# Transposing attention weights on VectorE and by transfers instead of on TensorE

## The chip, the cores and the metric

The kernel runs on one core of a Trainium2 chip. Its time is the device time of one execution, in microseconds (us). Three runs of the kernel before took 1422.08, 1422.11 and 1425.74 us; the median is 1422.11 us. One execution was also profiled: every instruction on the five engines (PE is TensorE, PEld its weight loads, DVE is VectorE, ACT is ScalarE, POOL is GpSimd) and on SyncE (SP), which here only issues transfers.

## The reference

Three layers follow one another. The attention pools keys and values over 8 positions, so each head has 576 queries and only 72 keys:

```
k_p = k.reshape(B, H, 72, 8, D).mean(axis=3)        # B = 8, H = 8, D = 64
v_p = v.reshape(B, H, 72, 8, D).mean(axis=3)
scores = (q @ k_p.T) / 8
attn = exp(scores - scores.max(-1)); attn = attn / (attn.sum(-1) + 1e-9)
x = attn @ v_p                                       # then 4608 tokens x 512
x = softplus(x @ w_in) @ w_out                       # 512 -> 2048 -> 512
# then: tokens with x @ w_skip > 0 go through one of 8 experts (512 -> 1024 -> 512),
# weighted by its gate, and are added to x; the others pass unchanged
```

## The kernel before, in words

**Groups.** The 4608 tokens are worked in nine groups of 512 (`NG = 9`, `G = 512`). A batch has 576 tokens, so a group holds a piece of one batch or pieces of two: 64 + 448 tokens in group 1, 128 + 384 in group 2, 192 + 320 in group 3, and so on to 448 + 64 in group 7; groups 0 and 8 lie in one batch. For group g the main loop (L738 to L765) goes through 16 columns c of the hidden layer: `p1` makes twelve matmuls `h` of 512 columns (L665) and the softplus on ACT and DVE, `p2`, two columns later, makes twelve matmuls `y` (L686 to L688). Matmuls are split into a high and a low part, three where one would do.

**Units.** The attention of group g + 1 is worked beside the main loop of group g, in four units, one per pair of heads. A unit is a generator (`unit`, L518); each `yield` ends one of its steps. `Feed.tick` (L645) advances every unit that runs by one step; it is called twice per column c, so a tick is twelve matmuls long, and a new unit starts every six ticks. The steps of a unit: load queries `q` and keys `k` (L533, L534); two ticks later pool the keys (L543), copy them into the two diagonal blocks of `kbd` (L550, L551), and multiply: scores `s` (L554) have queries on the partitions, up to six tiles of 64 to 128 queries per unit, each 144 wide (72 keys of two heads). DVE takes maxima and subtracts (L567, L568), ACT makes the exponential (L574), DVE sums and inverts (L575 to L577), POOL multiplies (L578). This lies in `q`'s own buffer. Then the weights have to stand with the keys on the partitions, as the product with the values needs them: PE transposes each tile and head into PSUM (`tr`, L606) and ACT copies the two halves to `et` (L608). Two ticks later PE makes `o` (L614), which ACT and DVE split into `xh` and `xl` (L616, L617). The values are pooled (L589) and transposed (`pv`, L595) on the way.

**Order.** A scheduler turns the program into one fixed list per engine; each engine works its list in order, so an instruction that waits holds up all behind it. SP's list holds all plain transfers: `k`, `q`, `v`, the gating rows `w9b` (L103), which wait for buffers that DVE's products `junk` (L118) free, and the stores `x2d` of finished rows (L155), which wait for the gate that DVE and POOL make at the end of `finish` (L106). `junk`, nine per row tile, 36 per group, runs beside the units of the second next group. There are two buffers for `q`, one each for `kv`, `et` and `vr`, and two PSUM banks (`ps_a`) for `s`, `pv`, `tr` and `o`.

**The tail.** After the last group the experts are worked in blocks of 256 rows (L803 on). There each block's rows are turned by DVE in 32x32 blocks and by 16 transfers from SBUF to SBUF (`spread`, L375 to L383), the only place of this kernel that does so.

Of the kernel before, what the change touches and what calls it, by code (L numbers as in the profile page):

```python
# [9 lines left out]
F32 = mybir.dt.float32  # L10
# [4 lines left out]
AF = mybir.ActivationFunctionType  # L15
ALU = mybir.AluOpType
AX = mybir.AxisListType
# [3 lines left out]
P = 128  # L21
# [4 lines left out]
SP = 72  # L26
G = 512
T = G // 128
# [6 lines left out]
def tile_kernel(ctx, tc, qT, kT, vT, wbits, w9, w1, w2, out):  # L35
    nc = tc.nc
# [23 lines left out]
    ident = const.tile([P, P], F32, name="ident")  # L60
# [358 lines left out]
    with ExitStack() as ph:  # L419
        pp = ph.enter_context(tc.tile_pool(name="pp", bufs=5))  # L420
# [6 lines left out]
        ps_a = ph.enter_context(tc.tile_pool(name="ps_a", bufs=2, space=PSUM))  # L427
# [3 lines left out]
        kbd = []  # L431
        for i in range(2):
            t = ep.tile([P, 2 * SP], F32, name=f"kbd{i}")
# [80 lines left out]

        pooled = {}
        count = [0]

        def unit(hp, part, xh, xl, first):  # L518

            pieces, n = [], 0  # L520
            for b, r0, rn, c0 in part:
                nt = -(-rn // P)
                if rn % nt:
                    nt += 1
                pieces.append((b * 4 + hp, r0, rn, c0, nt, rn // nt, n))
                n += nt
            assert n <= 6
            qe = room("q", G if first else 12 * SP, first)
            k = None
            for u, r0, rn, c0, nt, tp, n0 in pieces:  # L530
                if u not in pooled:
                    k = room("kv", 576, first)
                    nc.sync.dma_start(out=k, in_=kT[u])  # L533
                nc.sync.dma_start(out=qe[:, c0:c0 + rn], in_=qT[u, :, r0:r0 + rn])  # L534
            yield
            yield

            banks = [ps_a.tile([P, 512], F32, tag="pa", name="s") for _ in range(-(-n // 3))]
            parts = []
            for u, r0, rn, c0, nt, tp, n0 in pieces:  # L540
                if u not in pooled:
                    kp = pp.tile([P, SP], F32, tag="kp", name="kp")
                    nc.vector.tensor_reduce(kp, k.rearrange("p (s w) -> p s w", w=8), AX.X, ALU.add)  # L543
                    v = room("kv", 576, first)
                    nc.sync.dma_start(out=v, in_=vT[u])
                    pooled[u] = (kp, v, None)
                kp = pooled[u][0]
                kb = kbd[count[0] % 2]
                count[0] += 1
                nc.scalar.activation(out=kb[0:64, 0:SP], in_=kp[0:64, :], func=AF.Copy)  # L550
                nc.scalar.activation(out=kb[64:128, SP:2 * SP], in_=kp[64:128, :], func=AF.Copy)  # L551
                for t in range(nt):
                    i = n0 + t
                    nc.tensor.matmul(banks[i // 3][:tp, i % 3 * 144:(i % 3 + 1) * 144],  # L554
                                     lhsT=qe[:, c0 + t * tp:c0 + (t + 1) * tp], rhs=kb, start=True, stop=True)
                i = n0
                while i < n0 + nt:
                    j = min(n0 + nt, (i // 3 + 1) * 3)
                    parts.append((i, j, tp))
                    i = j  # L560
            e = (k if first else qe)[:, :n * 2 * SP].rearrange("p (a k) -> p a k", k=SP)
            st = room("st", 24 if first else 36, first)
            mx, sm, rc = (st[:, i * 2 * n:(i + 1) * 2 * n] for i in range(3))
            for i, j, tp in parts:
                s3 = banks[i // 3][:tp, i % 3 * 144:(i % 3 + j - i) * 144].rearrange("p (a k) -> p a k", k=SP)
                m = mx[:tp, 2 * i:2 * j]
                nc.vector.tensor_reduce(m, s3, AX.X, ALU.max)  # L567
                nc.vector.tensor_tensor(out=e[:tp, 2 * i:2 * j], in0=s3,  # L568
                                        in1=m.unsqueeze(2).to_broadcast([tp, 2 * (j - i), SP]),
                                        op=ALU.subtract)  # L570
            for u, r0, rn, c0, nt, tp, n0 in pieces:
                h = slice(2 * n0, 2 * (n0 + nt))
                ep_ = e[:tp, h]
                nc.scalar.activation(out=ep_, in_=ep_, func=AF.Exp, scale=1.0 / 64)  # L574
                nc.vector.tensor_reduce(sm[:tp, h], ep_, AX.X, ALU.add)  # L575
                nc.vector.tensor_scalar_add(sm[:tp, h], sm[:tp, h], 1e-9)
                nc.vector.reciprocal(rc[:tp, h], sm[:tp, h])  # L577
                nc.gpsimd.tensor_tensor(out=ep_, in0=ep_, op=ALU.mult,  # L578
                                        in1=rc[:tp, h].unsqueeze(2).to_broadcast([tp, 2 * nt, SP]))
            yield  # L580
            yield
            if not first:
                yield
            vr = None
            for u, *_ in pieces:
                kp, v, vp = pooled[u]
                if vp is None:
                    vr = room("vr", SP, first)
                    nc.vector.tensor_reduce(vr, v.rearrange("p (s w) -> p s w", w=8), AX.X, ALU.add)  # L589
            yield  # L590
            for u, *_ in pieces:
# [7 lines left out]
            if not first:  # L599
                yield  # L600
            et = room("et", 2 * G, first).rearrange("p (a k) -> p a k", a=2)[:SP]
            for h in range(2):
                tr = ps_a.tile([P, 512], F32, tag="pa", name="tr")
                for u, r0, rn, c0, nt, tp, n0 in pieces:
                    for t in range(nt):
                        nc.tensor.transpose(tr[:SP, c0 + t * tp:c0 + (t + 1) * tp],  # L606
                                            e[:tp, 2 * (n0 + t) + h, :], ident[:tp, :tp])
                nc.scalar.activation(out=et[:, h, :], in_=tr[:SP, :], func=AF.Copy)  # L608
            yield
            yield  # L610
            o = ps_a.tile([P, 512], F32, tag="pa", name="o")
            for u, r0, rn, c0, nt, tp, n0 in pieces:
# [4 lines left out]
            nc.vector.scalar_tensor_tensor(out=xl[:, hp, :], in0=o, scalar=0.125,  # L617
                                           in1=xh[:, hp, :].bitcast(F32), op0=ALU.mult, op1=ALU.subtract)

        X = {}  # L620

        def units_of(g):
            xh = xp.tile([P, 4, G], F32R, tag="xh", name="xh")
            xl = xp.tile([P, 4, G], F32R, tag="xl", name="xl")
            X[g] = (xh, xl)
            part = []
            t0 = g * G
            while t0 < (g + 1) * G:
                n = min((g + 1) * G, (t0 // 576 + 1) * 576) - t0
                part.append((t0 // 576, t0 % 576, n, t0 - g * G))  # L630
                t0 += n
            return [unit(hp, part, xh, xl, g == 0) for hp in range(4)]

        jobs, ends = [], []

# [142 lines left out]
        t = xp.tile([P, 4 * G], F32, tag="xl", name="xg1")  # L778
# [4 lines left out]
        g = NG - 1  # L783
# [171 lines left out]
```

## Time and profile before

| | |
|---|---|
| median of three runs | 1422.11 us (1422.08 to 1425.74) |
| the profiled execution | 1414.45 us, span of its instructions 1412.6 us |
| granted TensorE clock, mean over the span | 0.993 of full speed |
| busy in the span | PE 97%, PEld 81%, DVE 61%, ACT 45%, POOL 23% |
| transfers | 124.73 MB in 70752 packets |

The span is the time from the first to the last instruction of the profiled execution; 1.85 us lie around it. Its time is 7.66 us under the median of the three runs. Each row of a view gives an engine, a line of the kernel, the operation, the tiles as out<-in, the shapes and times; a wait is named by what ended it. A matmul's own duration holds its passage through the array, so that the durations of matmuls overlap: what one costs is read from the distance of starts.

### The profile page before, as it was taken

Reading aid. Unit: us, or ns where it says so; the run is one execution under the profiler, and the core shown is the slowest. Engines: PE = TensorE matmul, PEld = TensorE weight load, DVE = VectorE, ACT = ScalarE, POOL = GpSimd, SP = SyncE. Lnnn points to the kernel's source line nnn. Section 1 sums busy time; section 2 is a strip of 40 time slices with the busy share of each in tenths; the row PEclk is TensorE's granted clock in tenths of the full one; section 3 lists DMA queues with packets and bytes.
Section 4 is the critical chain, followed back from the end, with each engine's and each line's share of the span. In section 5 each row is a group of like instructions: output and inputs, shape, how many; then the busy total and the mean of one; then the engine's idle time right before and its main releaser. Section 6 shows DMA issues by size and latency. Waiting matters only on the chain. (4 is left out here: it accounts for less than half of the span.)

```text
span 1412.6 us, 21524 instructions
## 1 busy us (share of the span) xinstructions
PE 1366.5 (97%) x7290; PEld 1137.4 (81%) x7290; DVE 861.7 (61%) x2055; ACT 639.6 (45%) x1168; POOL 322.7 (23%) x370
## 2 busy tenths in 40 slices
PE   5899999999999999999999999999999999999986
PEld 3667877787877888778778878888998998989985
DVE  7897684784783883973963954844563532326263
ACT  6986555545554554555555454462111111114141
POOL 2011021021111121121121020234342443424332
PEclk9999999999999999999999999999999999999998
DMA  8813131131140230230220210423323222324272
GB/s 290 300 63 92 56 108 41 55 108 33 55 117 25 60 111 25 71 100 26 82 73 9 75 38 11 146 76 89 99 79 98 65 65 65 90 63 168 65 271 70
DMA packets 70752, 124.73 MB, mean 88 GB/s; under 512 B 21941, under 2 KB 37941, under 8 KB 68064
## 3 DMA queue, kind: packets, MB, share of 16 engines
q1 hardware_dynamic: 52896, 86.05, 19.7%
q0 software_dynamic: 17728, 37.13, 8.3%
q8 instruction: 61, 1.00, 0.3%
q14 instruction: 67, 0.55, 0.1%
HBM read 166.67 MB, written 29.67 MB: 139 GB/s over the span
## 5 line engine op out<-in xcount | busy, mean ns | idle before, releaser
L665 PE MATMUL h<-xh,wt 128*128 128x512 f32 x1152 | 388.5, 398 | 5.6 <-DVE a L671 5.0
L665 PEld LDWEIGHTS h<-xh,wt 128*128 128x128 f32 x1152 | 216.4, 188 | 62.9 <-issue 11.0
L118 DVE CUSTOM_DVE_ANT_0 junk<-rows,w9b 128x512 bf16<-128x512 f32 x324 | 234.4, 723 | 9.3 <-ACT rows L112 3.7
L838 PE MATMUL h<-xt,w1h 128*128 128x256 f32 x1280 | 227.9, 282 | 3.8 <-ACT w1h L403 3.0
L686 PE MATMUL y<-wt,gh 128*128 128x512 f32 x576 | 229.7, 399 | 0.0
L665 PE MATMUL h<-xl,wt 128*128 128x512 f32 x576 | 226.1, 392 | 0.0
L688 PE MATMUL y<-wt,gl 128*128 128x512 f32 x576 | 224.7, 390 | 0.0
L687 PE MATMUL y<-wt,gh 128*128 128x512 f32 x576 | 224.5, 390 | 0.0
L671 DVE SCALAR_TENSOR_TENSOR a<-h,a 128x512 f32<-128x512 f32 x144 | 99.0, 687 | 174.6 <-ACT a L670 174.4
L838 PEld LDWEIGHTS h<-xt,w1h 128*128 128x128 f32 x1280 | 197.5, 189 | 6.2 <-ACT w1h L403 3.8
L668 ACT ACTIVATE a<-h 128x512 f32<-128x512 f32 x144 | 86.1, 598 | 233.3 <-PE h L665 208.9
L578 POOL TENSOR_TENSOR q<-q,st 64x144 f32<-64x144 f32 (+7 forms) x60 | 64.2, 1078 | 541.0 <-DVE st L577 167.6
L842 ACT ACTIVATE hs<-h 128x512 fp32r<-128x512 f32 x80 | 47.5, 598 | 298.6 <-PE h L838 224.2
L838 PE MATMUL h<-xt,w1l 128*128 128x256 f32 x640 | 180.4, 282 | 1.4 <-DVE w1l L404 0.8
L673 ACT ACTIVATE gh<-a 128x512 fp32r<-128x512 f32 x144 | 91.0, 632 | 125.0 <-DVE a L671 124.4
L686 PEld LDWEIGHTS y<-wt,gh 128*128 128x128 f32 x576 | 108.2, 188 | 24.9 <-issue 1.0
L665 PEld LDWEIGHTS h<-xl,wt 128*128 128x128 f32 x576 | 108.5, 188 | 23.5 <-issue 2.9
L688 PEld LDWEIGHTS y<-wt,gl 128*128 128x128 f32 x576 | 108.1, 188 | 23.4 <-issue 0.7
L675 DVE TENSOR_TENSOR gl<-a,gh 128x512 fp32r<-128x512 f32 x144 | 100.2, 696 | 40.6 <-ACT gh L673 39.8
L687 PEld LDWEIGHTS y<-wt,gh 128*128 128x128 f32 x576 | 108.3, 188 | 20.6
L838 PEld LDWEIGHTS h<-xt,w1l 128*128 128x128 f32 x640 | 122.9, 192 | 1.8 <-DVE w1l L404 1.0
L864 PE MATMUL y<-w2h,hs 128*128 128x512 f32 x304 | 118.4, 390 | 1.2 <-DVE hs L843 1.2
(191 smaller groups left out, 1907.1 us busy)
## 6 DMA issues: line engine op xcount, KB each, us to landing
w9b<-w SPq DMA_DIRECT2D x81, 256.0 KB
raw<-wbits SPq DMA_DIRECT2D x12, 1024.0 KB
x2d<-rows SPq DMA_DIRECT2D x36, 260.0 KB
kv<-kT SPq DMA_DIRECT2D x28, 288.0 KB
kv<-vT SPq DMA_DIRECT2D x28, 288.0 KB
xm<-misc SPq DMA_DIRECT2D x160, 32.0 KB
misc<-misc SPq DMA_DIRECT2D x144, 32.0 KB
raw<-wbits SPq DMA_DIRECT2D x8, 512.0 KB
```

The costliest lines, as they stand in the source:

```text
L118: nc.vector.tensor_tensor_reduce(out=ws["junk"], in0=rows[t][:, :D], in1=w9b[e], scale=1.0, scalar=0.0, op0=ALU.mult, op1=ALU.add, accum_o ...
L578: nc.gpsimd.tensor_tensor(out=ep_, in0=ep_, op=ALU.mult, in1=rc[:tp, h].unsqueeze(2).to_broadcast([tp, 2 * nt, SP]))
L665: nc.tensor.matmul(h, lhsT=l, rhs=r[:, kk, :], start=n == 0, stop=n == 11)
L668: nc.scalar.activation(out=a, in_=h, func=AF.Abs)
L671: nc.vector.scalar_tensor_tensor(out=a, in0=h, scalar=0.0, in1=a, op0=ALU.max, op1=ALU.add)
L673: nc.scalar.activation(out=gh, in_=a, func=AF.Copy)
L675: nc.vector.tensor_tensor(out=gl, in0=a, in1=gh.bitcast(F32), op=ALU.subtract)
L686: nc.tensor.matmul(y, lhsT=th, rhs=wh, start=c == 0, stop=False)
L687: nc.tensor.matmul(y, lhsT=th, rhs=wl, start=False, stop=False)
L688: nc.tensor.matmul(y, lhsT=tl, rhs=wh, start=False, stop=c == 15)
L838: nc.tensor.matmul(h[:, f2, :], lhsT=l, rhs=r[:, kk, :], start=n == 0, stop=n == 11)
L864: nc.tensor.matmul(y, lhsT=hl[:, f, js], rhs=ws["w2h"][:, f, :], start=False, stop=f == 7)
```

## The change

Group 0 keeps the old way (`unit0`). For groups 1 to 8 the unit works four tiles of 128 queries whatever the pieces are: where a piece ends inside a tile, that tile's scores come from two matmuls with 64 rows each. Each tile and head has 96 columns, of which 72 hold weights and POOL sets 24 to zero. DVE then transposes the whole buffer in place, in 32x32 blocks, 128 x 768 elements in one instruction. A block then has the right content on the wrong partitions, so twelve transfers per unit, issued by SP, bring blocks of the same key range to their partitions in `et`: four bands of 32 source partitions times three key ranges of 32, 32 and 8 keys, each with eight runs of 32 elements (128 bytes) per partition. PE's transposes and ACT's copies of these units are gone. The output step comes five ticks after the transposition; before it came two ticks after the transposes on PE.

```diff
-            et = room("et", 2 * G, first).rearrange("p (a k) -> p a k", a=2)[:SP]
-            for h in range(2):
-                tr = ps_a.tile([P, 512], F32, tag="pa", name="tr")
-                for u, r0, rn, c0, nt, tp, n0 in pieces:
-                    for t in range(nt):
-                        nc.tensor.transpose(tr[:SP, c0 + t * tp:c0 + (t + 1) * tp],
-                                            e[:tp, 2 * (n0 + t) + h, :], ident[:tp, :tp])
-                nc.scalar.activation(out=et[:, h, :], in_=tr[:SP, :], func=AF.Copy)
...
+        def unit(hp, us, xh, xl):
+            qe = room("q", 2 * T * 96, False)
...
+            for u, r0, rn, c0 in us:
+                kb = keys(u, k, lambda: room("kv", 576, False))
+                c = c0
+                while c < c0 + rn:
+                    t, p0 = divmod(c, P)
+                    m = min(P - p0, c0 + rn - c)
+                    nc.tensor.matmul(banks[t // 2][p0:p0 + m, t % 2 * 144:(t % 2 + 1) * 144],
+                                     lhsT=qe[:, c:c + m], rhs=kb, start=True, stop=True)
+                    c += m
...
+            e = qe.rearrange("p (a k) -> p a k", k=96)
+            nc.gpsimd.memset(e[:, :, SP:], 0.0)
+            shares(e[:, :, :SP], sm, rc)
+            yield
+            yield
+            yield
+            nc.vector.transpose(out=qe, in_=qe)
+            et = room("et", 2 * G, False)
+            src = qe.rearrange("p (a k r) -> p a k r", k=3, r=32)
+            dst = et.rearrange("p (a q r) -> p a q r", q=4, r=32)
+            for q in range(4):
+                for kb, n in enumerate((32, 32, 8)):
+                    nc.sync.dma_start(out=dst[32 * kb:32 * kb + n, :, q], in_=src[32 * q:32 * q + n, :, kb])
+            vr = room("vr", SP, False)
+            sums(us, vr)
+            yield
+            values(us, vr)
+            yield
+            yield
+            yield
+            yield
+            output(us, et.rearrange("p (a k) -> p a k", a=2)[:SP], hp, xh, xl)
```

`keys`, `shares`, `sums`, `values` and `output` hold the code of the old unit's steps, one instruction where there was one per piece.

PE's list before, in the main loop of group 2, where the first unit of group 3 is transposed (`y` and `h` are the main loop's matmuls, `tr` the transposes, those of one shape in one row):

```order
L686 MATMUL y_2403<-wt_181,gh 128x512
L687 MATMUL y_2403<-wt_181,gh 128x512
L688 MATMUL y_2403<-wt_181,gl 128x512
L606 MATMUL tr<-ident,q 72x96 x2
L606 MATMUL tr<-ident,q 72x80 x4
...
L665 MATMUL h<-xh,wt_553 128x512
L665 MATMUL h<-xl,wt_553 128x512
```

The same place in PE's list now:

```order
L721 MATMUL y_2348<-wt_181,gh 128x512
L722 MATMUL y_2348<-wt_181,gh 128x512
L723 MATMUL y_2348<-wt_181,gl 128x512
L700 MATMUL h<-xh,wt_547 128x512
L700 MATMUL h<-xl,wt_547 128x512
```

The transposes between `y` and `h` are gone and nothing of the attention stands there.

SP's list before, in the main loop of group 2, where the rows of group 1 are stored (`w9b` are gating rows, `kv` keys or values, `x2d` the stores):

```order
L103 DMA w9b<-w 128x512
L545 DMA kv<-vT 128x576
L103 DMA w9b<-w 128x512 x2
L155 DMA x2d<-rows 128x520 x4
L533 DMA kv<-kT 128x576
L534 DMA q<-qT 128x256 x2
```

The same place in SP's list now (`et` are the new transfers):

```order
L522 DMA kv<-vT 128x576
L644 DMA et<-q 32x8x32 x2
L644 DMA et<-q 8x8x32
...
L644 DMA et<-q 32x8x32
L155 DMA x2d<-rows 128x520 x4
...
L609 DMA kv<-kT 128x576
```

The four stores, which used to stand alone, now stand among the twelve transfers of one unit, the third of the group.

## Rows read from the trace of the kernel before

**Rows 1.** Busy time of the engines over the span, from the page

```profile
PE 1366.5 (97%) x7290; PEld 1137.4 (81%) x7290; DVE 861.7 (61%) x2055; ACT 639.6 (45%) x1168; POOL 322.7 (23%) x370
```

**Rows 2.** Windows view: PE, PEld, DVE, ACT, POOL busy; clock, DMA share, GB/s

```profile
150.00:200.00 50.00, 49.01 (x242) 39.57 (x241) 44.65 (x122) 28.98 (x62) 3.98 (x4) 1.00 0.26 77
```

**Rows 3.** Waits of PE: engine, line, what ended the wait, total us, times, longest

```profile
PE o L614 <- DVE q L568: 5.2, 9, 1.2
```

**Rows 4.** PE's transposes: count, shortest/median/longest ns, first and last start, forms

```profile
L606 PE MATMUL tr<-ident,q x304: 230/259/291, 54.0 to 846.2; 128*72 128x128 f32 x64, 112*72 112x112 f32 x32, 80*72 80x80 f32 x32, 96*72 96x96 f32 x16
```

**Rows 5.** Timeline of PE, twelve matmuls apart: start us, duration us, instruction

```profile
305.49 0.39 PE L686 MATMUL y<-wt,gh 128*128 128x512 f32 x1
...
308.20 0.39 PE L665 MATMUL h<-xh,wt 128*128 128x512 f32 x1
```

**Rows 6.** Timeline of PE around transposes of 8, 12 and 10 tiles

```profile
169.21 0.39 PE L688 MATMUL y<-wt,gl 128*128 128x512 f32 x1
169.44 1.03 PE L606 MATMUL tr<-ident,q 128*72 128x128 f32 x8
...
170.55 0.39 PE L665 MATMUL h<-xl,wt 128*128 128x512 f32 x1
...
313.55 0.39 PE L688 MATMUL y<-wt,gl 128*128 128x512 f32 x1
313.77 1.05 PE L606 MATMUL tr<-ident,q 96*72 96x96 f32 x12
...
314.94 0.39 PE L665 MATMUL h<-xl,wt 128*128 128x512 f32 x1
...
681.62 0.39 PE L688 MATMUL y<-wt,gl 128*128 128x512 f32 x1
681.85 1.41 PE L606 MATMUL tr<-ident,q 112*72 112x112 f32 x10
...
683.53 0.40 PE L665 MATMUL h<-xl,wt 128*128 128x512 f32 x1
```

**Rows 7.** Timeline of PE around the scores of six tiles

```profile
317.23 0.39 PE L665 MATMUL h<-xh,wt 128*128 128x512 f32 x1
317.45 1.63 PE L554 MATMUL s<-kbd,q 128*96 128x144 f32 x12
...
319.15 0.40 PE L687 MATMUL y<-wt,gh 128*128 128x512 f32 x1
```

**Rows 8.** Timeline of PE: scores of two other units

```profile
296.58 1.63 PE L554 MATMUL s<-kbd,q 128*96 128x144 f32 x12
...
379.22 1.15 PE L554 MATMUL s<-kbd,q 128*128 128x144 f32 x8
```

**Rows 9.** Timeline of POOL: the last multiplication of the same two units

```profile
304.51 3.11 POOL L578 TENSOR_TENSOR q<-q,st 96x288 f32<-96x288 f32 x2 [17.76 <-ACT xh L616]
...
386.87 0.93 POOL L578 TENSOR_TENSOR q<-q,st 128x288 f32<-128x288 f32 x1 [0.87 <-DVE st L577]
```

**Rows 10.** DVE's block transposition in the tail: busy us, mean ns, idle before

```profile
L378 DVE STREAM_TRANSPOSE misc<-xg 128x512 f32<-128x512 f32 x38 | 24.8, 690 | 14.0 <-DVEq L823 5.5 <-DMA misc<-misc 4.0 <-DMA xg<-x2d,ids 1.4
```

**Rows 11.** The tail's transfers on SP: shortest/median/longest ns of an issue

```profile
L383 SPq DMA_DIRECT2D xm<-misc x160: 507/589/2146, 991.4 to 1401.1; - x160
```

**Rows 12.** Timeline of SP: one block's 16 transfers

```profile
991.40 10.03 SPq L383 DMA_DIRECT2D xm<-misc  x16
```

**Rows 13.** A stretch in which SP issues only such transfers

```profile
1016.00:1018.00 2.00, 2.00 (x11) 1.65 (x10) 0.67 (x2) 0.00 (x0) 0.00 (x0) 1.00 0.20 53
```

**Rows 14.** Timeline at the start: first load, and who uses it

```profile
0.80 0.40 SPq L533 DMA_DIRECT2D boot_kv<-kT  x1
...
3.61 0.75 DVE L543 TENSOR_REDUCE kp<-boot_kv 128x72 f32<-128x576 f32 x1 [2.31 <-DMA boot_kv<-kT]
```

**Rows 15.** Timeline of SP: stores of a group's rows

```profile
311.22 1.80 SPq L155 DMA_DIRECT2D x2d<-rows  x4
```

**Rows 16.** The stretch in which those stores and a key load move

```profile
311.00:317.00 6.00, 6.00 (x37) 5.03 (x35) 2.96 (x7) 3.58 (x7) 2.26 (x6) 1.00 0.74 239
```

More of the change, by code (lines that the diff above doesn't have):

```diff
@@ L516, in tile_kernel @@
         count = [0]
[L518 to L529, printed above, removed]
-            for u, r0, rn, c0, nt, tp, n0 in pieces:
[L531 to L551, printed above, removed]
-                for t in range(nt):
[L553 to L585, printed above, removed]
@@ new lines, in keys @@
+        def keys(u, k, kv):
+            if u not in pooled:
+                kp = pp.tile([P, SP], F32, tag="kp", name="kp")
+                nc.vector.tensor_reduce(kp, k.rearrange("p (s w) -> p s w", w=8), AX.X, ALU.add)
+                v = kv()
+                nc.sync.dma_start(out=v, in_=vT[u])
+                pooled[u] = (kp, v, None)
+            kp = pooled[u][0]
+            kb = kbd[count[0] % 2]
+            count[0] += 1
+            nc.scalar.activation(out=kb[0:64, 0:SP], in_=kp[0:64, :], func=AF.Copy)
+            nc.scalar.activation(out=kb[64:128, SP:2 * SP], in_=kp[64:128, :], func=AF.Copy)
+            return kb
@@ L586, in unit, with shares, sums @@
+        def shares(e, sm, rc):
+            nc.scalar.activation(out=e, in_=e, func=AF.Exp, scale=1.0 / 64)
+            nc.vector.tensor_reduce(sm, e, AX.X, ALU.add)
+            nc.vector.tensor_scalar_add(sm, sm, 1e-9)
+            nc.vector.reciprocal(rc, sm)
+            nc.gpsimd.tensor_tensor(out=e, in0=e, op=ALU.mult,
+                                    in1=rc.unsqueeze(2).to_broadcast([P, 2 * T, SP]))
+        def sums(us, vr):
+            for u, *_ in us:
                 kp, v, vp = pooled[u]
@@ L587, in unit, with values @@
                 if vp is None:
-                    vr = room("vr", SP, first)
                     nc.vector.tensor_reduce(vr, v.rearrange("p (s w) -> p s w", w=8), AX.X, ALU.add)
-            yield
-            for u, *_ in pieces:
+        def values(us, vr):
+            for u, *_ in us:
                 kp, v, vp = pooled[u]
@@ L598, in unit, with output @@
                     pooled[u] = (kp, v, vp)
[L599 to L610 removed]
+        def output(us, et, hp, xh, xl):
             o = ps_a.tile([P, 512], F32, tag="pa", name="o")
[L612 removed]
+            for u, r0, rn, c0 in us:
                 for h in range(2):
@@ L618, in unit, with unit0 @@
                                            in1=xh[:, hp, :].bitcast(F32), op0=ALU.mult, op1=ALU.subtract)
+        def unit0(hp, us, xh, xl):
+            (u, r0, rn, c0), = us
+            q, k = room("q", G, True), room("kv", 576, True)
+            nc.sync.dma_start(out=k, in_=kT[u])
+            nc.sync.dma_start(out=q, in_=qT[u, :, r0:r0 + rn])
+            yield
+            yield
+            banks = [ps_a.tile([P, 512], F32, tag="pa", name="s") for _ in range(2)]
+            kb = keys(u, k, lambda: room("kv", 576, True))
+            for t in range(T):
+                nc.tensor.matmul(banks[t // 3][:, t % 3 * 144:(t % 3 + 1) * 144],
+                                 lhsT=q[:, t * P:(t + 1) * P], rhs=kb, start=True, stop=True)
+            e = k.rearrange("p (a k) -> p a k", k=SP)
+            st = room("st", 24, True)
+            mx, sm, rc = (st[:, i * 8:(i + 1) * 8] for i in range(3))
+            for b, (i, j) in enumerate(((0, 3), (3, 4))):
+                s3 = banks[b][:, :(j - i) * 144].rearrange("p (a k) -> p a k", k=SP)
+                m = mx[:, 2 * i:2 * j]
+                nc.vector.tensor_reduce(m, s3, AX.X, ALU.max)
+                nc.vector.tensor_tensor(out=e[:, 2 * i:2 * j], in0=s3, op=ALU.subtract,
+                                        in1=m.unsqueeze(2).to_broadcast([P, 2 * (j - i), SP]))
+            shares(e, sm, rc)
+            yield
+            yield
+            vr = room("vr", SP, True)
+            sums(us, vr)
+            yield
+            values(us, vr)
+            et = room("et", 2 * G, True).rearrange("p (a k) -> p a k", a=2)[:SP]
+            for h in range(2):
+                tr = ps_a.tile([P, 512], F32, tag="pa", name="tr")
+                for t in range(T):
+                    nc.tensor.transpose(tr[:SP, t * P:(t + 1) * P], e[:, 2 * t + h, :], ident)
+                nc.scalar.activation(out=et[:, h, :], in_=tr[:SP, :], func=AF.Copy)
+            yield
+            yield
+            output(us, et, hp, xh, xl)
@@ L631, in units_of @@
                 t0 += n
-            return [unit(hp, part, xh, xl, g == 0) for hp in range(4)]
+            return [(unit if g else unit0)(hp, [(b * 4 + hp, *r) for b, *r in part], xh, xl) for hp in range(4)]
         jobs, ends = [], []
```

28 lines of the change are left out of this document (added).

## The prediction

> **What bounds the kernel now.** I read the page's busy times first, then the windows of the main loop, then the waits of PE, and last the timelines of single units. PE is busy for 1366.5 of 1412.6 us [rows 1]; in a stretch of 50 us of the main loop it works 49.01 us at the full clock of 2.4 GHz (1.00) [rows 2]. Of all waits of PE, the attention's output step `o` causes 5.2 us in nine waits, for the PSUM bank that DVE empties after the next unit's scores [rows 3]. So in the main loop a matmul less is time less, and an engine beside PE costs only when PE comes to something that isn't there. The reader is to see in the timeline that PE goes from `y` to `tr` to `h` without a gap [rows 6].
>
> **What PE loses.** Twelve matmuls of 512 columns start 2.71 us apart from the next twelve [rows 5]: 0.226 us each, and 2.71 us is also one tick. What a set of transposes costs is the distance from the last `y` before it to the second `h` behind it, less two such steps (the first `h` behind is late as well). For 8 transposes that is 170.55 - 169.21 - 0.45 = 0.89 us, for 12 it is 314.94 - 313.55 - 0.45 = 0.94, for 10 with 112 rows 683.53 - 681.62 - 0.45 = 1.46 [rows 6]. Groups 2, 4, 6 and 8 have 8 transposes per unit, 3 and 5 have 12, 1 and 7 have 10; with four units per group that is 4 x 38 x 2 = 304, the count in the trace [rows 4]. The sum: 4 x (4 x 0.89 + 2 x 0.94 + 2 x 1.46) = 33.4 us.
>
> Scores lose a little: 12 records (six tiles, two passes each) cost 319.15 - 317.23 - 0.45 = 1.47 us [rows 7], 0.12 us a record. In groups 3 and 5 the six tiles become five matmuls, eight units times two records: 2.0 us. In groups 1 and 7 there are five before and now; I count nothing, though their odd shapes may gain too.
>
> The bank waits of 5.2 us [rows 3]: before, `o` followed the next unit's scores after about twelve matmuls; in the new order there are 24 between them in groups 2 to 8, so DVE gets a tick more. I count all 5.2 as gone; the least is 0. PE's gain is then 33.4 + 2.0 + 5.2 = 40.6 us, if nothing comes late.
>
> **What is added, and where it lies.** DVE's transposition isn't in this stage of the trace; the tail has it with 512 columns at 690 ns [rows 10], so 768 columns are put at 690 x 768 / 512 = 1.04 us; from below 0.69. 32 of them are 33 us of DVE, which in the busiest stretch works 44.65 of 50 us [rows 2]; against that stand the reductions and subtractions that come once per bank instead of once per piece, and I count the two as even. DVE now waits at the transposition for POOL in its own list; behind it stand the softplus of the main loop, whose matmuls alternate with `y` so that PE asks for the result only two ticks (5.4 us) or more later. POOL has a small fill more, and is idle three quarters of the time [rows 1]. ACT loses its 64 copies, which nothing waited for. None of these is on PE's path.
>
> The transfers are what can be late. From the start of a unit's scores to its `o` PE now has 96 matmuls of the main loop, 96 x 0.226 = 21.7 us, its own scores and those of the next unit, 8 x 0.12 = 1.0 each, and the `o` of the unit before, about as much (an estimate, eight short matmuls like the scores'): the deadline is 24.7 us after the scores begin. Against it:
> - Scores to the end of POOL's multiplication: 386.87 + 0.93 - 379.22 = 8.6 us in a unit of four tiles, 304.51 + 3.11 - 296.58 = 11.0 us in one of six [rows 8, 9]. All units have four tiles now; I take 9, and keep 11.
> - DVE: at most one product of 0.7 us in the way, then 1.04 us.
> - Twelve issues on SP. In the tail 16 transfers of the same kind took 10.03 us, 0.627 each [rows 12]: 7.5 us. An issue there took 0.507 to 2.146, 0.589 in the middle [rows 11]: 6.1 to 25.8 us for twelve. I take 7.5, the mean of a run of 16.
> - The last one's way: the first load of the program is issued at 0.80 and used at 3.61 [rows 14]: 2.8 us, for nine times the bytes.
>
> That is 9 + 0.7 + 1.04 + 7.5 + 2.8 = 21.0 us, up to 23.0 from the slow end of the softmax: 1.7 to 3.7 us before the deadline. The engines behind SP hold it too: while the tail's transfers go, 20% of 16 engines are busy [rows 13], 0.20 x 16 x 0.627 = 2.0 us of engine time for 32 pieces of 1 KB, at most 63 ns a piece. A unit has 2304 pieces of 128 bytes; at 63 ns they are 9.1 us on each of 16 engines, at an eighth of it (by bytes) 1.1 us. Even 9.1 is 1.6 more than the issues, inside the margin.
>
> One unit per group has less room. In SP's order four stores of `x2d` stand among its transfers. Before, they were issued at 311.22, 14.6 us after that unit's scores at 296.58 [rows 8, 15]; with the transposition ahead of the gate on DVE that is 15.6. Then 1.80 for the stores, seven transfers behind them 4.4, and 2.8 of way: 24.6 against 24.7. The stores' bytes, 4 x 128 x 520 x 4 = 1.06 MB, at 239 GB/s [rows 16] 4.5 us, lie in the same queues and can put the end off by 0 to 4.5. Seven such units (groups 2 to 8) cost 0 to 30 us; I take 0.7 each, 5 us, since most of those bytes move while SP issues. The four units of group 1 share the queues with the weights' loads, and I allow them the same 0 to 4.5 each and count nothing.
>
> **Sum.** 40.6 - 5 = 35.6 us less. The profiled execution would go from 1414.45 to about 1378.9; the median of the runs stands 7.66 us above it, and I carry that over: 1386.5, say 1386 us. What PE does in the tail stays, only earlier.
>
> **Rivals.**
> A, the third unit of every group is late in full, because SP's list stalls among its transfers: 4.5 us x 7 = 31, and with group 1 another few; also part of the 5.2 us stays. The gain shrinks to between 5 and 25 us, 1397 to 1417. For it: the sum above ends 0.1 us from the deadline. Against: in the other units there is room, and the stores' bytes run beside SP's issues.
> B, slower: a transfer of 128-byte pieces takes longer than one of 1 KB pieces, at the issue or in the engines. It decides from the point where twelve take 7.5 + 3.7 = 11.2 us, 0.93 each; every unit then waits at `o` for the excess, since the next unit's scores stand behind it in PE's list. At twice the tail's price, 1.25 each or 15 us, it is 3.8 x 32 = 122 us of waiting against 40.6: 1422 + 81 = 1503. For it: 256 pieces per transfer instead of 32, and issues up to 2.1 us [rows 11]. Against: the key loads with 128 pieces were issued in 0.40 us [rows 14], less than the 0.589 of the tail's 32, so pieces don't set the issue there; and in time of the engines 63 ns is a price for eight times the bytes.
> C, PE's time isn't given back: DVE, with 33 us more in stretches at 44.65 of 50, delays the softplus and PE waits there; the gain is used up, 1418 to 1426. Against: the reductions that go, and 5 us of slack.
>
> The Trainium skill speaks for B: its page "DMA: Bandwidth & Descriptors", section "Specifications", says that below 512 bytes an engine reads, modifies and writes. Twice the price of a 1 KB piece would be 18 us per unit, 10.7 more than the issues, 32 x (10.7 - 3.7) = 224 us of waiting and a time of 1605 us; of B's chance 0.03 is for this. The same page, under "Why small descriptors are slow (HBM only)", exempts transfers within SBUF, and no run shown yet has such pieces.
>
> **How the numbers follow.** Forecast 0.57, A 0.23, B 0.13, C 0.07. About 0.3%, 4.3 us, is what a measurement can tell from no change. Forecast and A are faster, A with a little of its end in no change; C is no change or just over it: faster 0.79, same 0.07, slower 0.14. The forecast's own range is 1379 (40.6 gained, and a little of group 1's stalls) to 1396; with most of A it reaches 1376 to 1412, which leaves out the end of A, B and C.
>
> **What would show it.** Right: PE's records fewer by 304 + 16, no wait of PE at `o` for a transfer except in the third unit of a group, the twelve transfers issued in 7 to 8 us, DVE's transposition near 1.04 us, PE at 49 of 50 us in the main loop as before, and group 0's stage unchanged. Wrong: PE waiting at every `o` for `et`, with SP's issues above 0.93 us each or their landing far behind the last issue (B); waits at `o` once per group of 3 us and more, with `x2d` stores ahead (A); waits of PE at `h` for DVE's `a` (C).

## The result, and the profile after

The changed kernel took 1388.3 us (median of 4 runs, 1387.71 to 1388.97), the kernel before beside it 1422.09 (4 runs, 1421.27 to 1425.74). The ratio is 0.9758, with a 95% interval of 0.974 to 0.9775: faster by 33.8 us. The forecast was 1386 us, its range 1376 to 1412.

The page's busy times of the changed kernel, to be read against [rows 1]:

```profile
span 1386.9 us, 21423 instructions
...
PE 1338.3 (96%) x6970; PEld 1107.7 (80%) x6970; DVE 849.8 (61%) x1955; ACT 594.7 (43%) x1076; POOL 307.6 (22%) x374
...
q1 hardware_dynamic: 131744, 95.51, 23.9%
```

PE has 320 records fewer, 304 transposes and 16 halves of score matmuls, as counted. DVE's busy time is 12 us less, although 32 transpositions came in. The loads' queue carries 78,848 packets more (52,896 before) and takes 23.9% of the engines' time in place of 19.7%.

The gain is found by cutting the program at one matmul that both kernels have: the first `h` of the tail, the routed stage, at 958.3 us before and at 922.6 after. What lies ahead of it is 35.7 us shorter; the forecast's sum was 35.6. The main loop ahead of it is cut further at the first `h` matmul of each group. First the windows of before (PE, PEld, DVE, ACT, POOL busy; clock, DMA share, GB/s), then those of after, groups 0 to 3 and the whole loop:

```profile
31.40:146.50 115.10, 108.87 (x505) 79.30 (x506) 96.96 (x147) 96.25 (x160) 11.53 (x10) 0.98 0.44 154
146.50:248.00 101.50, 100.50 (x487) 80.72 (x487) 69.13 (x194) 54.38 (x109) 16.20 (x20) 1.00 0.23 68
248.00:352.60 104.60, 102.74 (x520) 83.16 (x519) 74.21 (x194) 55.04 (x109) 18.84 (x20) 1.00 0.23 66
352.60:453.90 101.30, 100.53 (x488) 81.17 (x487) 69.16 (x194) 54.11 (x109) 15.21 (x20) 1.00 0.24 69
...
31.40:958.30 926.90, 914.60 (x4385) 727.64 (x4385) 644.22 (x1635) 529.84 (x987) 147.53 (x169) 1.00 0.24 76
```

```profile
31.90:143.70 111.80, 105.88 (x462) 77.59 (x462) 94.03 (x127) 89.26 (x146) 7.08 (x10) 0.98 0.49 161
143.70:243.80 100.10, 98.36 (x460) 77.58 (x459) 71.27 (x181) 50.75 (x100) 15.36 (x20) 1.00 0.33 90
243.80:342.00 98.20, 98.20 (x464) 77.73 (x463) 68.94 (x178) 48.90 (x97) 15.23 (x20) 1.00 0.30 83
342.00:438.80 96.80, 96.80 (x456) 77.74 (x455) 68.73 (x178) 48.77 (x97) 14.87 (x20) 1.00 0.31 84
...
31.90:922.60 890.70, 882.30 (x4066) 697.54 (x4066) 632.71 (x1535) 485.39 (x895) 134.70 (x173) 1.00 0.31 90
```

The loop is 926.9 - 890.7 = 36.2 us shorter: PE works 914.60 - 882.30 = 32.3 us less, and its idle time falls from 12.3 to 8.4 us. In the stretches of groups 2 to 7 it has no idle time left. Each stretch holds the units of the next group. One thing crosses a border: in the changed kernel the last four `o` matmuls of group 1 (448 columns, at 143.97 us) stand behind the first `h` of the stretch of group 1, so about 1 us of work that before lay in the stretch of group 0 is counted there.

One unit of group 2 from its scores to `o` (all engines, then SP alone), the chain that the deadline was set against:

```profile
154.31 1.14 PE L620 MATMUL s<-kbd,q 128*128 128x144 f32 x8
...
160.60 1.59 POOL L536 TENSOR_TENSOR q<-q,st 128x576 f32<-128x576 f32 x1 [4.77 <-DVE st L535]
162.22 0.98 DVE L638 STREAM_TRANSPOSE q<-q 128x768 f32<-128x768 f32 x1 [1.04 <-POOL q L536]
163.27 8.20 SPq L644 DMA_DIRECT2D et<-q  x12
...
178.28 1.08 PE L559 MATMUL o<-et,vp 72*64 72x128 f32 x8
```

POOL ends 7.9 us after the scores' start, the transposition takes 0.98, the twelve issues end at 171.47, and `o` comes at 178.28, 24.0 us after the scores' start. The third unit of the same group has the four stores among its transfers; here are its scores on PE, its transposition, SP, and its `o`:

```profile
190.47 1.14 PE L620 MATMUL s<-kbd,q 128*128 128x144 f32 x8
...
204.16 0.96 DVE L638 STREAM_TRANSPOSE q<-q 128x768 f32<-128x768 f32 x1
205.19 1.27 SPq L644 DMA_DIRECT2D et<-q  x2
207.08 3.16 SPq L155 DMA_DIRECT2D x2d<-rows  x4
210.29 6.93 SPq L644 DMA_DIRECT2D et<-q  x10
...
218.79 1.08 PE L559 MATMUL o<-et,vp 72*64 72x128 f32 x8 [0.74 <-DMA et<-q]
```

The issues end at 217.22, and `o` starts 1.57 us behind that. This `o` is the only one of all 32 that waits for a transfer, 0.7 us, as the waits of PE in the main loop say:

```profile
PE h L700 <- DVE a L706: 3.4, 2, 2.0
PE s L620 <- ACT kbd L528: 2.5, 2, 2.4
PE h L700 <- DVE xl L562: 1.0, 1, 1.0
PE o L559 <- DMA et<-q: 0.7, 1, 0.7
```

### The profile page after: what moved, and what is told of

Read it like the earlier page. It is cut to its first block, busy times and chain, and to the rows that moved or that the text cites. A ratio compares the mean times of both kernels' runs of the same rounds, so it can differ in the third digit from the quotient of the medians.

```text
span 1386.9 us, 21423 instructions
## 1 busy us (share of the span) xinstructions
PE 1338.3 (96%) x6970; PEld 1107.7 (80%) x6970; DVE 849.8 (61%) x1955; ACT 594.7 (43%) x1076; POOL 307.6 (22%) x374
## 3 DMA queue, kind: packets, MB, share of 16 engines
q1 hardware_dynamic: 131744, 95.51, 23.9%
## 5 line engine op out<-in xcount | busy, mean ns | idle before, releaser
L700 PE MATMUL h<-xh,wt 128*128 128x512 f32 x1152 | 383.4, 394 | 3.7 <-DVE a L706 3.4
L118 DVE CUSTOM_DVE_ANT_0 junk<-rows,w9b 128x512 bf16<-128x512 f32 x324 | 222.5, 687 | 8.1 <-ACT rows L112 3.2
L897 PE MATMUL y<-w2h,hs 128*128 128x512 f32 x304 | 118.6, 390 | 1.6 <-ACTq L935 1.6
L899 PE MATMUL y<-w2h,hs 128*128 128x512 f32 x304 | 118.6, 390 | 0.8 <-DVE hs L878 0.8
```

Of the source, the lines that this page charges most:

```text
L118: nc.vector.tensor_tensor_reduce(out=ws["junk"], in0=rows[t][:, :D], in1=w9b[e], scale=1.0, scalar=0.0, op0=ALU.mult, op1=ALU.add, accum_o ...
L700: nc.tensor.matmul(h, lhsT=l, rhs=r[:, kk, :], start=n == 0, stop=n == 11)
L897: nc.tensor.matmul(y, lhsT=hh[:, f, js], rhs=ws["w2h"][:, f, :], start=f == 0, stop=False)
L899: nc.tensor.matmul(y, lhsT=hl[:, f, js], rhs=ws["w2h"][:, f, :], start=False, stop=f == 7)
```

## The experiments

The kernels were run on three chips, a set of kernels on each. The kernel before took 1424.03 us on the first (17 runs), 1414.33 on the second (9) and 1424.98 on the third (9); that difference is itself a result, told first. Main loops are compared from their first `h` to the first `h` of the routed stage.

**Both kernels again** (both on the first chip, the changed kernel on the third too), no edit.

> The kernel before, unchanged, to see how far its own executions differ. The gain up to the first matmul of the routed stage was 35.7 us by the two profiles (958.3 and 922.6 us), but the profiled ends differ by 25.8 us and the medians by 33.8. Theory 1: the routed stage of one kernel takes a different time from execution to execution, by 8 to 10 us, with waits that the profile puts down to 'issue'; then a second profile of the kernel before begins that stage at 958.3 within 0.5 us again, and where it ends above 1420 us it shows some 8 us of such waits behind 958. Theory 2: taking a profile of this kernel shortens it; then it ends at 1412.6 within 1 us again and shows no such waits, while the unprofiled times stay at 1422.

> The changed kernel, unchanged, beside the others on one chip. Theory 1 (the routed stage differs from execution to execution): the routed stage begins at 922.6 us within 0.5, and the time lies at 1388, or at 1378 to 1380 if that stage runs as short as in the first profile of the kernel before (454 us against 464). Theory 2 (profiling shortens the kernel before only): 1388 within 1 us in every execution.

> The changed kernel, unchanged, as the measure for the three beside it on the same chip. So far the routed stage (from the first matmul of h in it to the end) took 450 to 454 us in the kernels of one call and 462 to 465 in those of another, with 5 to 6 us of waits put down to 'issue' only in the second, whatever the kernel. Theory (that difference belongs to the chip): the routed stage begins at 922.0 to 922.6 us as before; where the kernel before takes some 1414 on this chip, this one takes 1377 to 1380 with none of those waits; where it takes 1424, 1387 to 1389. Rival (the changed kernel has the longer routed stage by itself): 1387 in either case.

Before took 1423.38 us, the changed kernel 1387.45 and 1389.02. The second profile of before reaches the routed stage at the same time (PE's timeline):

```profile
958.29 0.50 PE L838 MATMUL h<-xt,w1h 128*128 128x256 f32 x2 [0.74 <-ACT rows L112]
```

and in that stage it shows waits of PE that the first profile doesn't have:

```profile
PE h L838 <- issue: 5.6, 11, 0.8
```

The length of the routed stage (span less its start) in every profile:

```
kernel            start    span end   length   waits of h put down to issue
before (front)    958.3    1412.6     454.3    0
after             922.6    1386.9     464.3    5.8
first chip:  before_again 461.8 (5.6)   after_again 465.2 (5.1)
             uniform_pe   464.6 (5.7)   out_1_earlier 464.5 (5.8)
second chip: out_2_earlier 450.3 (0)    act_half 449.8 (0)
             split24       452.5 (0)    before_o_later 452.7 (0)
third chip:  after_third  464.6 (6.0)   no_move 463.4 (5.7)
             act_half_late 466.1 (5.8)  out_2_every5 465.8 (5.4)
```

The stage has the same code in all of them, and its length follows the chip, not the kernel: variants of the changed kernel took 450 to 453 us on the second chip, without such waits, so the longer stage isn't the changed kernel's own. That fits theory 1 in the form that the last expectation gave it, some 10 us that belong to the chip; each chip ran one set of kernels, at one time, so that it is the chip and not the occasion isn't shown. The first profile of before was, by its 454.3 us, of the quicker kind, and the runs of before at 1422 us of the slower; the changed kernel itself was never run on a chip of the quicker kind, so its 1377 to 1380 there were not seen. Within the slower kind the stage is 2.5 to 3.4 us longer in the changed kernel than in before (one profile of before); why was not tried.

**Four uniform tiles alone** (first chip): the transposition and the transfers are replaced by

```
-            nc.vector.transpose(out=qe, in_=qe)
-            ... (the twelve transfers)
+            for h in range(2):
+                tr = ps_a.tile([P, 512], F32, tag="pa", name="tr")
+                for t in range(T):
+                    nc.tensor.transpose(tr[:SP, t * P:(t + 1) * P], e[:, h * T + t, :SP], ident)
+                nc.scalar.activation(out=et[:, h, :], in_=tr[:SP, :], func=AF.Copy)
```

one tick behind `values`, and `o` follows two ticks later, as before.

> One part of the change alone: four uniform tiles of 128 rows in every unit of groups 1 to 8, but the weights transposed by TensorE as before (8 transposes and two ScalarE copies a unit), and no transfers. Theory: the gain is TensorE's own time. 256 transposes come back at 0.89 us for 8, that is 28.5 us, so 1388.3 + 28.5 = 1416.8; if the waits of o for a bank come back with the two extra banks, up to 1421. Against the kernel before, what is left is the 48 transposes and 16 score matmuls fewer, some 5 to 7 us. Rival: the uniform tiles carried most of the gain and the transposes were hidden; then under 1400.

It took 1416.5 us (0.9946 of before, 0.9932 to 0.996). Its main loop in one window, and then PE's waits at `o` for a bank:

```profile
31.30:949.00 917.70, 909.48 (x4322) 722.08 (x4322) 624.87 (x1503) 521.49 (x959) 135.24 (x173) 1.00 0.24 77
```

```profile
PE o L559 <- DVE q L630: 1.2, 3, 0.6
```

PE works 909.48 - 882.30 = 27.2 us more than in the changed kernel, for 256 transposes: 0.85 us for 8, where the sum had 0.89. The rival is out: of the 36.2 us the uniform tiles bring 9.2 and the transposes' leaving 27.0. (By the profiles of this chip alone, whose main loops take 927.3 us before and 890.0 after, it is 9.6 and 27.7.) The 1.2 us above are what is left here of the 5.2 us of bank waits.

**Before, with `o` one tick later** (second chip):

```
             yield
             yield
+            if not first:
+                yield
             o = ps_a.tile([P, 512], F32, tag="pa", name="o")
```

> The kernel before with o one tick later in groups 1 to 8, to measure the waits of o for a bank (5.2 us in 9 of the units) by themselves. Theory (o comes too soon behind the reductions that free its bank): most of the 5.2 us go, 1423.4 - 4.5 = 1419 (1417 to 1421). Rival (only fewer banks a unit help, or another wait takes their place): 1422 to 1425.

1408.86 against 1414.33 us on that chip (0.9961, 0.9947 to 0.9974). The routed stage began at 953.8, 4.5 us sooner than in before, and no wait of `o` for DVE is left. The bank waits were worth what [rows 3] said, and one `yield` takes them away without any change of the transposes.

**The moving left out** (third chip): `et` is filled with zeros by GpSimd in place of the transposition and the transfers, so the kernel leaves out the weights that `o` should read.

```
-            nc.vector.transpose(out=qe, in_=qe)
-            ... (the twelve transfers)
+            nc.gpsimd.memset(et[:SP], 0.0)
```

> The changed kernel without VectorE's transposition and without the twelve transfers of a unit: et is filled with zeros by GpSimd, so the weights that o reads are left out. This is what the change would be if the moving were free. Theory (transposition and transfers lie beside TensorE's work): the routed stage begins 0.7 us sooner, the one wait of o, up to 3 us: 919.3 to 921.6 for 922.3, the time within 0.3% of the changed kernel's. Rival (they cost TensorE something that its waits don't show, by the 4% more of the DMA engines' time or by VectorE's 31 us): sooner by 5 us or more.

1390.31 us against 1389.02 for the changed kernel. Its main loop, and its stretch of group 2:

```profile
32.30:923.50 891.20, 882.08 (x4065) 697.40 (x4065) 619.09 (x1503) 485.55 (x895) 166.61 (x204) 1.00 0.26 79
...
244.70:343.00 98.30, 98.30 (x464) 77.81 (x463) 67.32 (x174) 48.94 (x97) 19.80 (x24) 1.00 0.25 70
```

891.2 us, where the changed kernel beside it has 889.7; PE works 882.08 and 882.28 us. The routed stage began at 923.5, later than either theory had it: GpSimd's fills (32 of 0.95 us) come in the place of the moving, and the stretch of group 0 is 4 to 5 us longer than with it (115.6 for 111.8 and 110.9), which is mostly regained in the next (96.8 for 100.1 and 100.0). There the fills blur the comparison. In the stretches of groups 2 to 7 there is nothing to blur it: each is as long without the moving as with it, within 0.1 us (98.3 here and 98.2 in the changed kernel for group 2). The moving costs nothing there, and the rival is out.

**`o` one tick earlier** (first chip), one of the four `yield` between `values` and `output` taken out.

> The changed kernel with o one tick (2.71 us) earlier, to measure the slack of the transfers. From the end of the twelve issues to o there are 6.3 to 8.2 us in most units and 1.6 to 4.6 in the third units of the groups, whose stores stand among the transfers; 2.8 us are the landing. Theory (these slacks are all there is): most units still in time, the third units 1 to 4 us late, 13 us in all, so 1401 (1394 to 1410), with waits of TensorE at o for a transfer in about 7 units. Rival (the transfers land well before the issue's end plus 2.8 us, because early ones land while later ones are issued): 1388 with no such waits.

1392.12 us, and the routed stage at 925.9: 3.3 to 4.4 us later than in the changed kernel's three profiles: between the rival's 0 and the theory's 13, nearer to the rival. The waits are there but small; below are their sum, and two of the five:

```profile
PE o L559 <- issue: 2.5, 5, 1.1
```

```profile
526.56 1.08 PE L559 MATMUL o<-et,vp 72*64 72x320 f32 x8 [0.79 <-issue]
...
783.15 1.08 PE L559 MATMUL o<-et,vp 72*64 72x512 f32 x4 [1.15 <-issue]
```

Not all of this is the transfers' lateness. The wait at 526.56 ends 1.65 us behind the unit's last issue, and another of 0.19 at 213.12 ends 1.74 behind; these two, 1.0 us, fit the transfers. The other three, the 1.15 at 783.15 among them, end 2.4 to 4.3 us behind the last issue, too late for a transfer, and each 0.1 us after DVE has done the first subtraction of the next unit's scores: with one tick less `o` has the place that it has in the kernel before, one tick behind these scores, and some of its waits for a bank are back.

The records of single packets give the reason why the transfers cost so little: the last packet of nearly every unit ends 0.84 us after the twelfth issue. Where `o` waits for it, it starts 1.4 to 1.7 us behind that issue (1.57 in the changed kernel), not 2.8, so each unit had some 1.2 us more than I had counted.

**`o` two ticks earlier, and the two tries to mend it.** The first takes out two `yield` (second chip); the second starts the units every 5 ticks as well (third chip):

```
-                feed.start(units_of(g + 1), 6)
+                feed.start(units_of(g + 1), 5)
```

> The changed kernel with o two ticks (5.4 us) earlier. With o one tick earlier the last piece of a unit landed 0.84 us behind the end of its twelfth issue, and o waited where less than some 0.75 us were left; the last landing was 0.8 to 3.8 us ahead of o. Theory (the transfers end 2.7 us too late now, each in full on TensorE): first units late by 0 to 0.5 us, second by 0 to 2, third by 0 to 2.6, fourth by 0.6 to 2.6, 30 to 38 us in all, so 1425 (1405 to 1445), as slow as the kernel before. Rival (a stall at one o gives the next unit its time back): about 1400.

> The kernel with o two ticks earlier, with units started every 5 ticks in place of 6. With 6, o stands in the same tick as the next unit's scores, and these waited 9.2 us in 11 units for the reading of o's bank; the routed stage began at 942.0 for 922.3. Theory 1 (the loss is the shared tick: scores behind o wait for its bank): the waits of the scores go, and what is left are the late transfers, 5 to 10 us: 927 to 933. Theory 2 (the transfers' lateness in another guise): still 938 to 945.

The first took 1394.93 us where before takes 1414.33 (0.9863, 0.9848 to 0.9879), with a main loop of 910.3 us, 19.6 more than the changed kernel's 890.7. I had expected 37, all at `o`. Less than a third of it is there, as PE's waits show:

```profile
PE s L620 <- DVE xl L562: 9.2, 11, 1.4
PE h L698 <- DVE a L704: 6.3, 4, 2.3
PE o L559 <- DMA et<-q: 5.8, 3, 2.8
```

One place in PE's timeline shows why `s` waits for `xl`:

```profile
120.03 0.34 PE L559 MATMUL o<-et,vp 72*64 72x64 f32 x4
120.19 0.86 PE L620 MATMUL s<-kbd,q 128*64 128x144 f32 x6
```

Units start 6 ticks apart, and `o` now comes 6 ticks behind its own scores: in the tick of the next unit's scores. In this order they stand directly behind one another, and `s` waits till DVE has read a bank that `o` wrote (`xl`). With the units 5 ticks apart these waits are gone altogether, the main loop is 895.9 us, and the time 1394.38 beside 1389.02 for the changed kernel on that chip. Theory 1 of the second expectation holds; the routed stage began at 927.5.

**Half of the transfers on ScalarE's queue** (the first on the second chip with `o` two ticks earlier, the second on the third chip with `o` in its place):

```
-                    nc.sync.dma_start(out=dst[32 * kb:32 * kb + n, :, q], in_=src[32 * q:32 * q + n, :, kb])
+                    dma = nc.sync if q < 2 else nc.scalar
+                    dma.dma_start(out=dst[32 * kb:32 * kb + n, :, q], in_=src[32 * q:32 * q + n, :, kb])
```

> The changed kernel with o two ticks earlier and six of a unit's twelve transfers issued by ScalarE's queue, six by SP's. Theory (the one queue's issues in a row set when et is there): two rows of six take 4.1 us, the last piece lands 4.1 us sooner, which covers what o two ticks earlier lacks; 1390, up to 1420 if ScalarE's own work (an issue that waits for the transposition stands ahead of the softplus) comes late. Rival (the 16 DMA engines' work on the pieces sets it): as with o two ticks earlier and all on SP, about 1425.

> The changed kernel with six of a unit's twelve transfers issued by ScalarE's queue, and o where the changed kernel has it. With o two ticks earlier this split did not help: 25 us up to the routed stage, with 7.7 us of waits of h for the softplus. Theory 1 (the split costs nothing by itself, o's place did it): the routed stage begins at 922.3 within 1.5 us. Theory 2 (six issues a unit on ScalarE, each behind the wait for the transposition, hold up the softplus): 3 to 8 us later, with waits of TensorE for the softplus above the 3.4 us of the changed kernel.

The first took 1399.78 us (before 1414.33) with a main loop of 915.7, more than without the split. Both its theory and its rival fall: the transfers' end wasn't what `o` two ticks earlier lacked, and the split costs something itself. The second shows that by itself: 1400.84 us (1393.47 to 1402.02) beside 1389.02, the routed stage at 933.3, 11 to 12 us later, above even theory 2's 3 to 8. ScalarE's timeline in one unit, and then PE's:

```profile
208.31 0.23 ACT L134 ACTIVATE z<-z 128x32 f32<-128x32 f32 x1
210.26 4.15 ACTq L645 DMA_DIRECT2D et<-q  x6
214.51 0.60 ACT L704 ACTIVATE a<-h 128x512 f32<-128x512 f32 x1 [5.98 <-DMA x2d<-rows]
215.01 0.26 ACT L552 ACTIVATE vp<-pv 72x128 f32<-72x128 f32 x1
...
215.32 0.76 PE L620 MATMUL s<-kbd,q 128*128 128x144 f32 x4 [1.87 <-ACT vp L552]
```

ScalarE stands still from 208.54 to 214.51: until 210.22 for the transposition, then for its six issues. Behind them stand the softplus and the copy `vp`, and PE's next scores wait for `vp`. (The profile names a store of `x2d` as what ended the idle time; by the queue's own rows it is the issues.) All of PE's waits of this kind:

```profile
PE h L701 <- DVE a L707: 5.6, 5, 2.2
...
PE s L620 <- ACT vp L552: 5.0, 6, 1.9
```

Together they are 8.7 us more than in the changed kernel beside it (1.9 and 0), of the 11.7 that the main loop is longer (901.4 for 889.7).

**Each transfer in two** (second chip), the same pieces:

```
+                    for a in (slice(0, 4), slice(4, 8)):
+                        nc.sync.dma_start(out=dst[32 * kb:32 * kb + n, a, q], in_=src[32 * q:32 * q + n, a, kb])
```

> The changed kernel with each of the twelve transfers of a unit issued as two of half the pieces (24 issues, the same 2304 pieces of 128 bytes). Theory (a transfer costs its issue on SP, 0.61 to 0.68 us, whatever it carries): 24 issues take 16.4 us in place of 8.2, the last piece lands 8.2 us later, o waits 3 to 5 us in most units and 5 to 8 in the third ones, 130 us in all, so 1518 (1470 to 1570). Rival (the issue's time goes with the pieces): half a transfer takes half as long, 24 take 8.2 us, and the time stays at 1388.

1514.04 us (1.0703 of before, 1.0686 to 1.0719). SP's timeline has all 24 issues in a row; PE's `o` starts 0.59 us after the last one ends. (Its first matmuls read only the first head, whose last pieces go with the 23rd issue: by the single records `o` starts 1.3 us behind that one, and its matmuls of the second head 1.3 us behind the 24th.) First the timeline, then PE's waits, then the main loop and one stretch of it as windows:

```profile
171.83 16.78 SPq L645 DMA_DIRECT2D et<-q  x24
...
189.20 2.65 PE L559 MATMUL o<-et,vp 72*64 72x128 f32 x8 [5.04 <-DMA et<-q]
```

```profile
PE o L559 <- DMA et<-q: 55.5, 20, 5.8
...
PE o L559 <- issue: 10.4, 7, 3.0
```

```profile
31.30:1060.90 1029.60, 940.98 (x4065) 729.13 (x4065) 637.25 (x1535) 489.73 (x895) 137.22 (x173) 0.95 0.27 78
180.00:200.00 20.00, 14.91 (x56) 10.71 (x55) 14.91 (x40) 7.21 (x17) 1.47 (x1) 0.83 0.33 95
```

16.78 / 24 = 0.70 us for half the pieces, 8.20 / 12 = 0.68 for all: half the pieces make an issue no shorter, and the rival is out. The main loop is 1029.6 - 890.7 = 138.9 us longer, close to the 130 expected, but made up otherwise: PE's idle time grows from 8.4 to 88.6 us (66 of it at `o`, 14 at `s` for `kbd`), and its work from 882.3 to 941.0, for as many matmuls. Most of that work is the clock: 0.95 in the mean, worth 0.05 x 1029.6 = 51 us (an estimate), and 0.83 in the window that holds the 5.04 us of waiting, so for about a third of that window it was at 1.2 and not at 2.4 GHz.

## Why the prediction was right

- **The bound.** Right from group 2 on: the changed kernel's PE has no idle time in the stretches of groups 2 to 7, and what was taken from it is time. The moving is hidden there, as the kernel without it shows; for the stretches of groups 0 and 1 no run shows it cleanly.
- **PE's loss** was counted at 33.4 + 2.0 = 35.4 us, and is 32.3; against the second profile of before, whose stretch of group 0 holds 1.5 us more work, it is 33.8. By experiment: 5.1 us of work (6.5 by that second profile) go with the 48 transposes and 16 score records that the uniform tiles save (6.9 counted: 4.9 and 2.0), 27.2 with the other 256 transposes (28.5 counted). From the stretch of group 2 on 27.1 us went for 26.0. The stretches of groups 0 and 1, which hold the units of groups 1 and 2, lost 3.0 and 2.1 us for 5.8 and 3.6 counted; the `o` at 143.97 makes the first loss 1 us too large and the second 1 us too small. So the shortfall lies in the stretch of group 0. There PE idles some 6 us in either kernel, and [rows 6] was the wrong place to read the price from.
- **The bank waits** were counted at 5.2 us. None is left in the changed kernel, and the tick alone gave before 4.5. PE's idle time fell by only 3.9 us, because other waits came, all in the stretches of groups 0 and 1: 2.5 us for `kbd` (2.4 in the kernel without the moving too), 1.0 for `xl` and 0.7 for the transfers.
- **The third units** were counted at 5 us and cost 0.7, in one of the seven. That the margin was nearly right is luck: 24.6 against 24.7 us was counted, and in that unit it was 28.3 against 27.6, with errors on both sides. Against it: its transposition came 13.7 us behind its scores (9.7 counted), ten transfers stood behind the stores there, not seven (6.93 us for 4.4), and the stores took 3.16 us in place of 1.80. For it: `o` was due behind 106 matmuls of the main loop, not 96, and could start 1.6 us behind the last issue in place of 2.8. The 2.8 came from [rows 14] and ran from the start of an issue (2.4 from its end), for a load from memory of nine times the bytes; for a transfer within the chip it was the wrong row. Rival A did not come.
- **The other units.** In the unit shown the softmax took 7.9 us (9 counted), the transposition 0.98 (1.04), the twelve issues 8.2 (7.5, 0.68 each for 0.63), and the deadline was 24.0 (24.7). With 1.6 us behind the last issue the weights were there after 18.7 us: five to spare, where I had counted 1.7 to 3.7. One tick less leaves 2.6 there and nothing in some third units; `o` one tick earlier shows about 1 us of such waits.
- **The sum** of 35.6 us beside the measured 35.7 is closer than its terms. PE's work fell by 32.3 for 35.4 counted, the bank waits went as counted, 4.2 us of other waits came for the 5 counted at the third units, and waits that nobody had counted went, 1.6 us for the softplus and some less. The mechanism is right; the agreement to 0.1 us is luck.
- **Rival B** did not come: an issue of 0.68 us stays below its 0.93. Its mechanism came once the issues were doubled, most `o` wait; but the 139 us by which that main loop is longer don't confirm its size. Its 122 us of waiting were for 15 us of issues. For the 16.78 measured the same sum gives (16.78 - 11.2) x 32 = 179 us, and 66 were seen at `o`, the rest being other waits and the clock. The engines' price was far below the bound: in the stretch that holds all pieces of one unit, 163 to 172.5 us, 16 engines are 0.19 busy, 0.19 x 16 x 9.5 = 28.9 us for 2304 pieces: some 12 ns for 128 bytes, where I had allowed up to 63, or 8 by bytes.

```profile
163.00:172.50 9.50, 9.50 (x47) 7.92 (x46) 9.32 (x26) 3.18 (x6) 0.00 (x0) 1.00 0.19 31
```

  The Trainium skill's rule of a price below 512 bytes ("DMA: Bandwidth & Descriptors", section "Specifications") is not seen in these transfers as the prediction had priced it, at twice the 63 ns of a 1 KB piece; the same page's exemption for transfers within SBUF ("Why small descriptors are slow (HBM only)") is what the trace agrees with, though by the byte 12 ns for 128 bytes is still one and a half times 63 ns for 1 KB.
- **Rival C** did not come: PE waits 3.4 us for the softplus, 5.0 before.
- **The offset of 7.66 us** was carried over without a reason. The likely one is that the profiled execution of before came from a quicker chip than the runs. So the forecast for the runs came right, since the main loop's gain comes off on either kind; the 1378.9 for the profiled execution did not, it took 1388.66. The 2.3 us between 1386 and 1388.3 lie in the routed stage, which no edit touches.

## What to carry to other kernels

Where PE is without gaps, taking a matmul away gives its spacing, and the spacing must be read from the stretch that it is taken from. A step moved off PE is then a question of one deadline, and the sum of the chain behind it should take each duration from the nearest kind of transfer: the count of issues on one queue set it here (24 in place of 12 made the main loop 139 us longer, with the same pieces), not the pieces. When an order leaves slack, look what stands in the tick to which something is moved: a bank shared with the next unit cost more than the data being late.

## What the runs showed of the hardware that was not expected

- Twelve transfers within SBUF, eight of 256 pieces of 128 bytes and four of 64, hold SP's queue for 0.68 us each; cut into 24 of half the pieces, 0.70 each. The last packet ends 0.84 us behind the issue, and a matmul that waits for it starts 1.3 to 1.7 us behind.
- The routed stage of one code takes 450 to 453 us on one chip and 462 to 466 on two others, with 5 to 6 us of waits of PE on these in which the profile shows nothing that it waits for.
- Waits of up to 5.8 us at 27 of 32 `o` cost much again by the clock: 80 us more of idle time (66 at `o`) and 59 us more of work for the same matmuls, at a mean granted clock of 0.95, in the kernel with 24 transfers.
- Six issues on ScalarE's queue, behind their wait for VectorE, kept ScalarE from its own work for 5.98 us in the unit shown, and the kernel became 11.8 us slower (1400.84 for 1389.02).
